# Softmax normalisation on VectorE, stored weight parts, and another order of products in a paired feed-forward layer

## The chip, the cores and the metric

The kernel runs on one core of one Trainium2 chip, in one launch. The metric is the device time of a whole execution in microseconds (us); the median of three runs is shown. All data is fp32. Matrix products run in the TensorE type `fp32r`, and to keep the precision each factor is split into a high part (the value rounded to `fp32r`) and a low part (the rest), so that one product of two factors is three matmuls: high by high, high by low, low by high.

## What is computed

Causal attention over 4 batches, 12 heads, 448 positions and 64 values a head, then a layer norm and a feed-forward layer with a residual:

```python
scores = scale * np.matmul(q, k.transpose(0, 1, 3, 2))
scores = np.where(mask, -1000000000.0, scores)        # mask: above the diagonal
attn = np.exp(scores - np.max(scores, axis=-1, keepdims=True))
attn = attn / (np.sum(attn, axis=-1, keepdims=True) + 1e-09)
x = heads_joined(np.matmul(attn, v))                  # (4, 448, 768)
xn = (x - mu) / np.sqrt(var + 1e-06) * g_ln
out = x + np.maximum(xn @ w_ch1, 0.0) @ w_ch2         # 768 -> 3072 -> 768
```

## The kernel before

All engines run in the order in which the code is written (`manual_schedule`); each engine works its own queue strictly in that order, and waits where an operand is not ready. Time is divided by hand into *slots*: slot s emits 18 feed-forward matmuls (half of a block of the generator `ffn`, one yield), preceded and followed by whatever the tables `pre`, `post` and `ahead` hold for that slot.

**Weights.** The weights arrive as 64-bit floats and are cut into units of 128x768; there are 48 units a batch (`ns`), used one a slot. For batch 0 a unit is loaded raw (`load_raw`), converted in two steps (`convert1` on ScalarE, `convert2` on VectorE, line 129), and kept in device memory as fp32 (`keep`). For batch 1 (slots 48 to 95) `load_full` reads it back. For either, `split1` (ScalarE, line 141) makes the high part `wh` and `split2` (VectorE, line 145) the low part `wl`, two slots and one slot ahead of the use. Each has four buffers.

**Attention.** Batch 0 runs ahead of the slots. Batches 1, 2 and 3 are laid under the slots of batches 0 and 1 by `STARTS`: a pair of heads p begins at its slot t0 and runs scores (TensorE), running maximum and mask (VectorE, line 277), `exps` (ScalarE), `norm`, transposes, and the product with v. `norm` forms 1/sum on VectorE (lines 302 and 303) and multiplies four triangular pieces of 112 rows by 112, 224, 448 and 336 with it (line 307), on GpSimd. Line 238 subtracts the high part of k on GpSimd.

**The pair.** Batches 2 and 3 go through the feed-forward layer together, with seven products for the eight of a 2x2 block product (the Winograd form of Strassen's scheme): the weights give the left factors A11, A12, A22 and the sums S1 to S4, the two batches give the right factors B11, B21, B22 and the differences T1 to T4. `LEFT` and `RIGHT` name which belong to products 1 to 7.

- `inputs(c)` makes the right factors of one of three chunks from the normalised inputs of both batches (`xg`): eight operations for `xg`, four subtractions t1 to t4, and for each of seven factors the high part on ScalarE and the low part on GpSimd or VectorE (`parts`, lines 534 and 535). It is called in slots 87, 90 and 93 (`PAIR` is 86).
- After slot 95 `run` goes over 30 blocks in six groups: two blocks of layer 1 (63 matmuls each, nine a product), then three of layer 2 (42 each, six a product). Product 4 of a layer-2 block is put behind the first product of the next block.
- `load` and `combine` bring a block's weights from device memory and form S1 to S4 on GpSimd (line 627), 15 and 11 products ahead. `weight` splits each of the seven left factors six products ahead (`AHEAD`), high part on ScalarE and low part on VectorE.
- A product accumulates in one of three PSUM banks of its block, A, X or Y. `after1` and `after2` do what follows: partial results are copied to SBUF (p1, p5, u2), added into banks, and in layer 1 turned by ReLU into the right factors of layer 2 (`hid`, high and low); in layer 2 they are added to the residual `xT`.

## Time and profile before

| | us |
|---|---|
| runs | 984.96, 985.91, 987.09; median 985.91 |
| profiled execution | 984.65 |
| its span, first to last instruction | 982.9 |
| busy in the span: TensorE | 887.1 |
| VectorE | 715.0 |
| ScalarE | 531.8 |
| GpSimd | 400.0 |
| mean granted TensorE clock | 0.975 |

An engine's busy time is the union of its instructions' spans. Matmuls overlap: one is shown with 0.37 us, while the next starts 0.20 us after it. So the pace is read from starts, and a wait from the idle time ahead of an instruction and what ended it. Busy shares are averages over stages with different limits, so the span is cut into stages.

### The profile page before, as it was taken

What the parts mean: (1) busy time and instruction counts of PE and PEld (TensorE: products, weight loads), DVE (VectorE), ACT (ScalarE), POOL (GpSimd) and SP (SyncE); (2) the same over time, 40 slices, a digit from 0 to 9 for tenths busy, and PEclk for the clock granted to TensorE, in tenths of its full rate; (3) what the DMA queues carried; (4) which work ended last, traced back from release to release, by engine and by line L of the source; (5) the groups of instructions that cost most, each with busy time, mean ns of one, the idle gap of its engine ahead of it and who ended that gap; (6) DMA issues with size and microseconds to landing.
All of it is one profiled execution on the core that took longest, in us unless ns stands there. A gap on an engine that the chain in (4) does not pass through costs nothing.

```text
span 982.9 us, 13419 instructions
## 1 busy us (share of the span) xinstructions
PE 887.1 (90%) x4662; PEld 757.8 (77%) x4662; DVE 715.0 (73%) x1341; ACT 531.8 (54%) x1176; POOL 400.0 (41%) x447
## 2 busy tenths in 40 slices
...
GB/s 249 320 47 141 170 260 283 287 291 290 245 252 148 194 186 112 112 112 111 123 127 33 85 81 11 52 54 54 42 66 43 54 54 38 70 43 55 54 44 112
DMA packets 35251, 125.51 MB, mean 128 GB/s; under 512 B 4080, under 2 KB 8688, under 8 KB 35184
## 3 DMA queue, kind: packets, MB, share of 16 engines
...
## 4 chain that ended last, share of the span: by engine, by line
PE 52%; DVE 26%; ACT 13%; issue 5%; DMA 3%; SPq 1%; POOL 0%; ACTq 0%; DVEq 0%; POOLq 0%
PE po L493 13%; PE ph L474 13%; DVE wp L535 6%; PE bX L667 6%; PE bY L667 4%; PE bA L667 4%; PE px L342 4%; DVE w L129 3%; PE sc L269 3%; PE pt L323 3%; DVE xT L734 2%; ACT wp L534 2%; DVE t L682 2%; DVE wl L145 2%; ACT P L291 1%
## 5 line engine op out<-in xcount | busy, mean ns | idle before, releaser
L307 POOL TENSOR_SCALAR P<-P,r 112x112 f32<-112x112 f32 (+3 forms) x176 | 110.3, 645 | 275.6 <-DVE r L303 259.4
L493 PE MATMUL po<-hh,wl 128*128 128x448 f32 x288 | 109.0, 379 | 29.7 <-DVE wl L145 29.7
L535 DVE TENSOR_TENSOR wp<-s,wp 128x256 fp32r<-128x256 f32 (+1 forms) x120 | 95.7, 799 | 34.4 <-ACT wp L534 32.2
L291 ACT ACTIVATE P<-P,nm 112x448 f32<-112x448 f32 (+3 forms) x176 | 91.8, 526 | 48.4 <-DVE nm L277 48.2
L493 PE MATMUL po<-hh,wh 128*128 128x448 f32 x288 | 109.5, 380 | 0.0
L493 PE MATMUL po<-hl,wh 128*128 128x448 f32 x288 | 108.1, 375 | 0.0
L474 PE MATMUL ph<-xh,wh 128*128 128x448 f32 x288 | 107.8, 374 | 0.0
L474 PE MATMUL ph<-xh,wl 128*128 128x448 f32 x288 | 106.0, 368 | 1.4 <-DVE wl L145 1.4
L474 PE MATMUL ph<-xl,wh 128*128 128x448 f32 x288 | 105.8, 367 | 0.8 <-POOL xl L409 0.8
L535 DVE TENSOR_TENSOR wp<-u,wp 128x256 fp32r<-128x256 f32 (+1 forms) x90 | 71.6, 796 | 35.5 <-ACT wp L534 35.5
L277 DVE CUSTOM_DVE_ANT_0 P<-sc,mask 112x448 f32<-112x448 f32 (+3 forms) x176 | 70.5, 443 | 30.3 <-PE sc L269 18.3
L493 PEld LDWEIGHTS po<-hh,wl 128*128 128x128 f32 x288 | 56.2, 195 | 36.8 <-DVE wl L145 31.9
L480 DVE SCALAR_TENSOR_TENSOR hl<-ph,hh 128x448 fp32r<-128x448 f32 x48 | 29.8, 622 | 69.7 <-ACT hh L479 69.7
L627 POOL TENSOR_TENSOR s<-u 128x256 f32<-128x256 f32 (+1 forms) x60 | 58.4, 973 | 53.1 <-DVE wp L535 25.3
L129 DVE SCALAR_TENSOR_TENSOR w<-w,bits 128x768 uint32<-128x768 uint32 x48 | 73.7, 1536 | 3.7 <-ACT bits L122 3.5
L667 PE MATMUL bY<-h,wp 128*128 128x448 f32 x216 | 54.3, 381 | 21.0 <-ACT fx L742 15.3
L667 PEld LDWEIGHTS bY<-h,wp 128*128 128x128 f32 x216 | 40.0, 189 | 29.6 <-ACT fx L742 17.6
L145 DVE TENSOR_TENSOR wl<-full,wh 128x768 fp32r<-128x768 f32 x48 | 61.2, 1279 | 1.6 <-ACT wh L141 1.6
L667 PE MATMUL bX<-h,wp 128*128 128x448 f32 x216 | 55.7, 381 | 6.8 <-DVE xT L734 6.8
L323 PE MATMUL pt<-ident,P 112*112 112x112 f32 x440 | 54.8, 261 | 7.1 <-DVE stat L358 3.9
L493 PEld LDWEIGHTS po<-hh,wh 128*128 128x128 f32 x288 | 56.3, 195 | 5.1
L323 PEld LDWEIGHTS pt<-ident,P 112*112 112x112 f32 x440 | 46.3, 133 | 17.3 <-ACT PT L326 3.6
...
## 6 DMA issues: line engine op xcount, KB each, us to landing
...
scratch<-w SPq DMA_DIRECT2D x48, 384.0 KB, 5.1
...
```

The costliest lines, as they stand in the source:

```text
L129: nc.vector.scalar_tensor_tensor(out=w, in0=w, scalar=3, in1=bits.pop(s), op0=ALU.logical_shift_left, op1=ALU.bitwise_or,)
L145: nc.vector.tensor_tensor(out=wl[s], in0=w32[s], in1=wh[s].bitcast(F32), op=ALU.subtract)
L277: nc.vector.tensor_tensor_reduce(out=self.t["P", p, h][:, OFF[i]:OFF[i + 1]], in0=pt[:, o:o + n], in1=mask[:, S - n:], op0=ALU.add, op1=AL ...
L291: nc.scalar.activation(out=pp, in_=pp, func=ACTF.Exp, scale=-1.0, bias=nm[:, x:x + 1], accum_out=self.t["sm", p, h][:, i:i + 1],)
L307: eng.tensor_scalar(out=pp, in0=pp, scalar1=r[:, i:i + 1], scalar2=1.0, op0=ALU.mult, op1=ALU.mult,)
L323: nc.tensor.transpose(pt[:, o:o + C], pp[:, a:a + C], ident[:C, :C])
L342: nc.tensor.matmul(px[D * h:D * h + D, C * j:], lhsT=vt[:, h, j, :], rhs=self.t.pop(("PT", p, h, j)), start=(j == 0), stop=(j == NC - 1),)
L474: nc.tensor.matmul(pm[y], lhsT=w[:, c * P:c * P + P], rhs=z[:, c, :], start=(c == 0 and i == 0), stop=(c == KC - 1 and i == 2),)
L493: nc.tensor.matmul(pm, lhsT=w[:, o:o + P], rhs=z[:, x, :], start=(x == 0 and i == 0), stop=(x == HF - 1 and i == 2),)
L535: eng.tensor_tensor(out=lo, in0=src, in1=hi.bitcast(F32), op=ALU.subtract)
L627: nc.gpsimd.tensor_tensor(out=v[out], in0=x, in1=y, op=op)
L667: nc.tensor.matmul(pm, lhsT=w, rhs=z, start=(new and c == 0 and i == 0), stop=(c == nk - 1 and i == 2), skip_group_check=True,)
```

## The change

Four things change.

1. `norm` multiplies on VectorE for batches 1 to 3 instead of GpSimd, and the attention of batches 2 and 3, with the pair's start, is two slots earlier.
2. Each rounded unit of slots 36 to 83 is also stored as its two parts (`keep_parts`, two DMAs). Units 84 to 95 are read back as parts (`load_parts`) instead of being read and split. In the pair the left factors A11, A12 and A22 are read as parts (`weight_parts`, one DMA) and only S1 to S4 are split.
3. The pair's inputs come in twelve portions, one in each of slots 84 to 95, instead of three lumps; B11 and B21 use the buffers of `xh` and `xl`.
4. In the pair product 1 accumulates in bank X with 6, 7 and 4; layer 1 keeps its differences in the banks A, Y and a fourth, Z, instead of SBUF; parts of the work behind products 3 and 4 are put off by one or two products (`then`); layer 2 adds each bank's running value into `xT` on VectorE, without copies. The products stand in another order.

The diff, cut (of functions that were rewritten mostly the new lines are shown; the old ones stand above):

```diff
-STARTS[2] = [32 + 4 * p for p in range(6)]
-STARTS[3] = [56 + 4 * p for p in range(6)]
+STARTS[2] = [30 + 4 * p for p in range(6)]
+STARTS[3] = [54 + 4 * p for p in range(6)]
-PAIR = 86
-LEFT = {1: "A11", 2: "A12", 3: "S4", 4: "A22", 5: "S1", 6: "S2", 7: "S3"}
+PAIR = 84
+KEEP0 = 36
+LEFT = {1: (0, 0), 2: (0, 1), 3: "S4", 4: (1, 1), 5: "S1", 6: "S2", 7: "S3"}
-ORDER1, ORDER2 = [1, 6, 5, 2, 7, 3, 4], [1, 5, 6, 3, 2, 7, 4]
+ORDER1, ORDER2 = [1, 2, 6, 5, 7, 3, 4], [1, 5, 6, 3, 7, 2, 4]
...
+    def load_parts(s):
+        for part, w, tag in ((0, wh, "wh"), (1, wl, "wl")):
+            t = sb.tile([P, UH], F32, tag=tag, name=tag, bufs=4)
+            nc.sync.dma_start(out=t, in_=kept[s % ns][:, part, :])
+            w[s] = t.bitcast(F32R)
+    def keep_parts(s):
+        for part, w in ((0, wh), (1, wl)):
+            nc.sync.dma_start(out=kept[s % ns][:, part, :], in_=w[s].bitcast(F32))
...
 
         put(ns, (open_late, None))
         for s in range(2 * ns):
+            if s >= ns + KEEP0:
+                put(s - 3, (load_parts, s))
+                continue
             t = (-EARLY + GAP * s, *ELAG) if s < early else (s - 4, 1, 2, 3)
             put(t[0] + t[3], (split2, s))
+            if s >= KEEP0:
+                put(s, (keep_parts, s))
...
-        rank = [open_late, split2, convert2, convert1, keep, load_raw, load_full, split1]
+        rank = [open_late, split2, convert2, convert1, keep, load_raw, load_full, keep_parts, load_parts, split1]
...
         def parts(self):
-            self.xh = xp.tile([P, KC, S], F32R, tag="xh", name="xh", bufs=1)
-            self.xl = xp.tile([P, KC, S], F32R, tag="xl", name="xl", bufs=1)
+            self.xh = sb.tile([P, KC, S], F32R, tag="xh", name="xh", bufs=1)
+            self.xl = sb.tile([P, KC, S], F32R, tag="xl", name="xl", bufs=1)
...
-            eng = nc.vector if self.b == 0 and p >= NDVE else nc.gpsimd
+            eng = nc.vector if self.b or p >= NDVE else nc.gpsimd
...
+            self.at[0].parts()
             self.xo = {
                 (op, part): self.xp.tile([P, KB, S], F32R, tag=f"x{op}{part}", name=f"x{op}{part}")
-                for op in RIGHT.values() for part in "hl"
+                for op in RIGHT.values() for part in "hl" if op not in ("B11", "B21")
             }
+            for k, op in enumerate(("B11", "B21")):
+                for part, t in (("h", self.at[0].xh), ("l", self.at[0].xl)):
+                    self.xo[op, part] = t[:, k * KB:(k + 1) * KB, :]
+            self.f = {}
...
+        def xg(self, c, k, j):
...
+            nc.vector.tensor_tensor(out=t, in0=a.xT[cc], in1=a.t["mb"], op=ALU.subtract)
+            nc.vector.scalar_tensor_tensor(
+                out=t, in0=t, scalar=g_sb[:, cc:cc + 1], in1=a.t["rb"], op0=ALU.mult, op1=ALU.mult,
+            )
...
+        def xsub(self, c, name, x, y):
+            self.f[c, name] = t = self.tmp(name)
+            nc.vector.tensor_tensor(out=t, in0=self.f[(c, *x)], in1=self.f[(c, *y)], op=ALU.subtract)
+        def xparts(self, c, op, x, eng):
+            self.parts(self.f[(c, *x)], self.xo[op, "h"][:, c, :], self.xo[op, "l"][:, c, :], eng)
+
         def inputs(self, c):
...
+            G, V = nc.gpsimd, nc.vector
+            return [
+                [(self.xg, c, 0, 0), (self.xparts, c, "B11", (0, 0), G), (self.xg, c, 0, 1)],
+                [(self.xg, c, 1, 1), (self.xsub, c, "t1", (0, 1), (0, 0)), (self.xsub, c, "t2", (1, 1), ("t1",)),
+                 (self.xparts, c, "T2", ("t2",), G)],
+                [(self.xg, c, 1, 0), (self.xparts, c, "B21", (1, 0), G), (self.xparts, c, "T1", ("t1",), V)],
+                [(self.xsub, c, "t3", (0, 1), (1, 1)), (self.xparts, c, "T3", ("t3",), G),
+                 (self.xsub, c, "t4", (1, 0), ("t2",)), (self.xparts, c, "B22", (1, 1), G),
+                 (self.xparts, c, "T4", ("t4",), V)],
+            ]
...
-            for n in range(len(self.items)):
-                self.todo.setdefault(n - AHEAD, []).append((self.weight, n))
-            self.u, self.s, self.w, self.bank, self.hid = {}, {}, {}, {}, {}
+            for n, (b, k) in enumerate(self.items):
+                if isinstance(LEFT[k], tuple):
+                    self.todo.setdefault(n - AHEAD, []).append((self.weight_parts, n))
+                else:
+                    self.todo.setdefault(n - AHEAD, []).append((self.weight, n))
...
+        def weight_parts(self, n):
+            b, k = self.items[n]
+            w, (i, kk) = self.width(b), LEFT[k]
+            s, o = self.unit(b, i)
+            o += kk * w
+            s, o = s + o // UH, o % UH
+            t = sb.tile([P, 2, w], F32, tag=("wh", "wl")[n % 2], name="wk", bufs=4)
+            nc.sync.dma_start(out=t, in_=kept[s][:, :, o:o + w])
+            self.w[b, k] = t.bitcast(F32R)
...
         def weight(self, n):
+            w, src = self.width(b), self.u[b][LEFT[k]]
+            self.w[b, k] = t = sb.tile([P, 2, w], F32R, tag=("wh", "wl")[n % 2], name="wp", bufs=4)
+            nc.scalar.activation(out=t[:, 0, :], in_=src, func=ACTF.Copy)
+            nc.vector.tensor_tensor(
+                out=t[:, 1, :], in0=src, in1=t[:, 0, :].bitcast(F32), op=ALU.subtract
+            )
...
-            name = {1: "A", 2: "A", 6: "X", 7: "X", 4: "X", 5: "Y", 3: "Y"}[k]
+            name = {1: "X", 2: "A", 6: "X", 7: "X", 4: "X", 5: "Y", 3: "Y"}[k]
-            (self.after1 if blk[0] == 1 else self.after2)(b, blk, k)
...
+            def rest(op, src, eng=V):
+                minus(lo(op), src, hi(op).bitcast(F32), eng)
+
+            def then(lag, f, *args):
+                self.later.setdefault(self.n + lag, []).append((f, args))
...
             if k == 1:
-                nc.scalar.copy(out=self.p1, in_=bank["A"])
+                self.p1 = self.tmp("p1")
+                copy(self.p1, X)
             elif k == 6:
-                V.tensor_tensor(out=bank["X"], in0=bank["X"], in1=self.p1, op=ALU.add)
                 self.u2 = self.tmp("u2")
-                nc.scalar.copy(out=self.u2, in_=bank["X"])
+                copy(self.u2, X)
+            elif k == 2:
+                plus(A, A, self.p1)
+                self.b11 = self.tmp("b11")
+                copy(hi("B11"), A, ACTF.Relu)
+                copy(self.b11, A, ACTF.Relu)
+                rest("B11", self.b11, G)
             elif k == 5:
-                nc.scalar.copy(out=self.p5, in_=bank["Y"])
-                V.tensor_tensor(out=bank["Y"], in0=bank["Y"], in1=self.u2, op=ALU.add)
...
+                self.p5 = self.tmp("p5")
+                copy(self.p5, Y)
+                plus(Y, Y, self.u2)
             elif k == 7:
+                Z = self.psum(b, "Z")
+                plus(Z, X, self.p5)
                 self.b22 = self.tmp("b22")
...
+                copy(hi("B22"), Z, ACTF.Relu)
+                copy(self.b22, Z, ACTF.Relu)
+                rest("B22", self.b22, G)
             elif k == 3:
...
+                relu_minus(A, Y, self.b11)
+                minus(Z, self.b22, A)
+                copy(hi("T1"), A)
+                copy(hi("T2"), Z)
+                relu_minus(Y, Y, self.b22)
+                rest("T1", A)
+                rest("T2", Z)
+                then(1, copy, hi("T3"), Y)
+                then(2, rest, "T3", Y)
             elif k == 4:
...
+                b21 = self.tmp("b21")
+                copy(b21, X, ACTF.Relu)
+                copy(hi("B21"), X, ACTF.Relu)
+                rest("B21", b21, G)
+                then(1, minus, Z, b21, Z)
+                then(1, copy, hi("T4"), Z)
+                then(2, rest, "T4", Z)
...
-            def add(i, j, src, eng):
...
+            def add(i, j, src):
                 m = 2 * blk[2] + i
                 t = self.at[j].xT[m]
-                eng.tensor_tensor(out=t, in0=t, in1=src, op=ALU.add)
+                nc.vector.tensor_tensor(out=t, in0=t, in1=src, op=ALU.add)
...
-            if k == 1:
-                nc.scalar.copy(out=self.p1, in_=bank["A"])
-            elif k == 5:
-                nc.scalar.copy(out=self.p5, in_=bank["Y"])
-            elif k == 6:
-                V.tensor_tensor(out=bank["X"], in0=bank["X"], in1=self.p1, op=ALU.add)
-                add(0, 1, bank["X"], V)
-                add(1, 1, self.p5, G)
-            elif k == 3:
-                add(0, 1, bank["Y"], V)
-            elif k == 2:
-                add(0, 0, bank["A"], V)
-            elif k == 7:
-                add(1, 1, bank["X"], V)
-            elif k == 4:
-                add(1, 0, bank["X"], V)
+            add(*{
+                1: (0, 0, X), 5: (1, 1, Y), 6: (0, 1, X), 3: (0, 1, Y), 7: (1, 1, X), 2: (0, 0, A), 4: (1, 0, X),
+            }[k])
 
...
             for n, (b, k) in enumerate(self.items):
                 self.product(b, k)
                 self.before(n)
+                self.n = n
+                (self.after1 if self.blocks[b][0] == 1 else self.after2)(b, self.blocks[b], k)
+                for f, args in self.later.pop(n, []):
+                    f(*args)
...
-                elif (s - PAIR) % 3 == 1 and (s - PAIR) // 3 < KB:
-                    pair.inputs((s - PAIR) // 3)
+                    steps = [x for c in range(KB) for x in pair.inputs(c)]
+                for f, *args in steps.pop(0) if steps else []:
+                    f(*args)
```

VectorE's queue where the pair's inputs begin to be made, before: the end of the first lump (`t`: t1 to t4; `xT2l`, `xT4l`: low parts), then the low parts of three feed-forward units.

```order
L544 SCALAR_TENSOR_TENSOR xg<-xg,g_sb,rb 128x448
L543 TENSOR_TENSOR xg<-xT,mb 128x448
L544 SCALAR_TENSOR_TENSOR xg<-xg,g_sb,rb 128x448
L554 TENSOR_TENSOR t_5793<-xg 128x448
L554 TENSOR_TENSOR t_5795<-xg 128x448
L554 TENSOR_TENSOR t_5805<-xg,t_5793 128x448
L554 TENSOR_TENSOR t_5807<-xg,t_5805 128x448
L535 TENSOR_TENSOR xT2l<-t_5805,xT2h 128x448
L535 TENSOR_TENSOR xT4l<-t_5807,xT4h 128x448
L145 TENSOR_TENSOR wl<-full,wh 128x768 x2
L497 TENSOR_TENSOR xT<-po,xT 128x448
L145 TENSOR_TENSOR wl<-full,wh 128x768
```

The same queue after, from the second portion on (`L513` is the feed-forward's addition, `L561` and `L562` make `xg`, `L568` the differences, `L556` low parts):

```order
L513 TENSOR_TENSOR xT<-po,xT 128x448
L561 TENSOR_TENSOR xg<-xT,mb 128x448
L562 SCALAR_TENSOR_TENSOR xg<-xg,g_sb,rb 128x448
L568 TENSOR_TENSOR t_5877<-xg 128x448
L568 TENSOR_TENSOR t_5879<-xg,t_5877 128x448
L561 TENSOR_TENSOR xg<-xT,mb 128x448
L562 SCALAR_TENSOR_TENSOR xg<-xg,g_sb,rb 128x448
L556 TENSOR_TENSOR xT1l<-t_5877,xT1h 128x448
L513 TENSOR_TENSOR xT<-po,xT 128x448
L568 TENSOR_TENSOR t_5937<-xg 128x448
L568 TENSOR_TENSOR t_5941<-xg,t_5879 128x448
L556 TENSOR_TENSOR xT4l<-t_5941,xT4h 128x448
```

The input operations now stand in short pieces between the feed-forward's additions, and no low parts of units stand behind them.

VectorE's queue where the second layer-1 block of a group ends and layer 2 begins, before (`wp`: low part of a left factor; `t<-bX,t` and `h<-bX,h`: T4 and B21 behind product 4; `bX<-bX,fx`, `xT`: layer 2):

```order
L535 TENSOR_TENSOR wp<-u_6613,wp 128x256
L682 SCALAR_TENSOR_TENSOR t_6863<-bX,t_6836 128x448
L682 SCALAR_TENSOR_TENSOR h_6111<-bX,h_6111 128x448
L535 TENSOR_TENSOR wp<-s,wp 128x256
L535 TENSOR_TENSOR wp<-u_6719,wp 128x256
L535 TENSOR_TENSOR wp<-u_6613,wp 128x256
L744 TENSOR_TENSOR bX<-bX,fx 128x448
L734 TENSOR_TENSOR xT<-xT,bX 128x448
L535 TENSOR_TENSOR wp<-s,wp 128x256
L734 TENSOR_TENSOR xT<-xT,bY 128x448
L535 TENSOR_TENSOR wp<-s,wp 128x256
L734 TENSOR_TENSOR xT<-xT,bA 128x448
```

The same place after (`L709`, `L714`: T1, T2, T3 behind product 3 and their low parts `h` and `hx`; `bZ`: T4; `L779`: additions into `xT`):

```order
L709 SCALAR_TENSOR_TENSOR bA<-bY,b_6388 128x448
L714 TENSOR_TENSOR bZ<-b_6442,bA 128x448
L709 SCALAR_TENSOR_TENSOR bY<-bY,b_6442 128x448
L714 TENSOR_TENSOR h_6235<-bA,h_6235 128x448
L714 TENSOR_TENSOR hx<-bZ,hx 128x448
L779 TENSOR_TENSOR xT<-xT,bX 128x448
L714 TENSOR_TENSOR hx<-bY,hx 128x448
L714 TENSOR_TENSOR bZ<-b_6479,bZ 128x448
L779 TENSOR_TENSOR xT<-xT,bY 128x448
L714 TENSOR_TENSOR h_6235<-bZ,h_6235 128x448
L660 TENSOR_TENSOR wp<-s,wp 128x256
L779 TENSOR_TENSOR xT<-xT,bX 128x448
```

The additions of layer 2 now begin between the low parts of T2, T3 and T4, and low parts of left factors are fewer.

ScalarE's queue from product 3 of the first layer-1 block to the first copy of the second block (`fx<-bA` of line 687, the copy p1), before:

```order
L534 ACTIVATE wp<-u_7534 128x384
L534 ACTIVATE h_6110<-t_7713 128x448
L534 ACTIVATE h_6110<-t_7714 128x448
L534 ACTIVATE h_6111<-t_7715 128x448
L534 ACTIVATE wp<-s 128x384
L719 ACTIVATE h_6110<-bX 128x448
L534 ACTIVATE h_6110<-t_7741 128x448
L534 ACTIVATE wp<-s 128x384
L687 COPY fx<-bA 128x448
```

The same place after (`p_7342<-bX` is the copy p1, `h_6234<-bZ` behind it the high part of T4):

```order
L706 ACTIVATE h_6234<-bA 128x448
L706 ACTIVATE h_6234<-bZ 128x448
L659 ACTIVATE wp<-s 128x384
L706 ACTIVATE b_7325<-bX 128x448
L706 ACTIVATE h_6234<-bX 128x448
L706 ACTIVATE h_6235<-bY 128x448
L706 ACTIVATE p_7342<-bX 128x448
L706 ACTIVATE h_6234<-bZ 128x448
```

The copy p1 moved ahead of the high part of T4, and one high part of a left factor is between instead of three.

## Rows read from the trace of the kernel before

**Rows 1.** By stage: us, busy of PE, PEld, DVE, ACT, POOL, PEclk, DMA share, GB/s
```profile
60.00:543.00 483.00, 465.89 (x2672) 400.46 (x2673) 340.90 (x708) 301.67 (x629) 148.71 (x179) 1.00 0.49 178
543.00:613.00 70.00, 43.49 (x197) 38.99 (x196) 47.57 (x57) 17.67 (x33) 31.83 (x24) 0.80 0.15 53
613.00:979.40 366.40, 327.89 (x1513) 286.44 (x1511) 285.12 (x435) 166.54 (x384) 183.51 (x177) 0.98 0.17 55
```

**Rows 2.** Timeline, TensorE in the pair (start, us, engine, line, op): pace
```profile
737.65 0.36 PE L667 MATMUL bX<-xT2h,wp 128*128 128x448 f32 x1
...
739.49 0.36 PE L667 MATMUL bY<-xT1h,wp 128*128 128x448 f32 x1
```

**Rows 3.** Timeline, TensorE between 546 and 613 us
```profile
546.60 0.45 PE L493 MATMUL po<-hh,wh 128*128 128x448 f32 x1
...
610.20 0.57 PE L493 MATMUL po<-hh,wh 128*128 128x448 f32 x1
...
610.57 0.57 PE L493 MATMUL po<-hl,wh 128*128 128x448 f32 x1
...
612.95 0.36 PE L667 MATMUL bA<-xB11h,wp 128*128 128x448 f32 x1
```

**Rows 4.** Waits of TensorE, 543 to 613 us: total, times, longest
```profile
PE po L493 <- DVE wl L145: 26.5, 3, 10.4
```

**Rows 5.** Waits of TensorE, 613 to 983 us
```profile
PE bY L667 <- ACT fx L742: 15.3, 6, 2.6
PE bA L667 <- ACT fx L687: 8.7, 6, 1.6
PE bX L667 <- DVE xT L734: 6.8, 13, 1.2
PE bY L667 <- DVE h L535: 5.7, 6, 1.0
```

**Rows 6.** Timeline, VectorE in the first input lump
```profile
560.68 1.55 DVE L535 TENSOR_TENSOR xT4l<-t,xT4h 128x448 fp32r<-128x448 f32 x1
```

**Rows 7.** Groups of the pair: busy us, mean ns of one, idle before
```profile
L535 DVE TENSOR_TENSOR wp<-u,wp 128x256 fp32r<-128x256 f32 (+1 forms) x90 | 71.6, 796 | 35.5 <-ACT wp L534 35.5
...
L734 DVE TENSOR_TENSOR xT<-xT,bA 128x448 f32<-128x448 f32 x18 | 11.0, 608 | 0.1
...
L682 DVE SCALAR_TENSOR_TENSOR t<-bY,b 128x448 f32<-128x448 f32 x24 | 14.7, 611 | 0.0
...
L535 DVE TENSOR_TENSOR h<-t,h 128x448 fp32r<-128x448 f32 x18 | 10.5, 610 | 0.0
...
L693 ACT COPY fx<-bY 128x448 f32<-128x448 f32 x12 | 6.4, 531 | 1.6 <-PE bY L667 1.6
```

**Rows 8.** DMA issues from 255 to 340 us: KB each, median us to landing
```profile
scratch<-w SPq DMA_DIRECT2D x11, 384.0 KB, 4.5
```

**Rows 9.** Timeline, VectorE at the border into layer 2
```profile
701.56 1.26 DVE L535 TENSOR_TENSOR wp<-s,wp 128x256 fp32r<-128x256 f32 x1 [1.69 <-ACT wp L534]
...
704.77 0.61 DVE L535 TENSOR_TENSOR h<-t,h 128x448 fp32r<-128x448 f32 x1
...
705.30 0.61 DVE L535 TENSOR_TENSOR hx<-t,hx 128x448 fp32r<-128x448 f32 x1
```

**Rows 10.** VectorE groups by shape, and by line (ns min/median/max), up to 545 us
```profile
L129 DVE SCALAR_TENSOR_TENSOR w<-w,bits 128x768 uint32<-128x768 uint32 x44 | 69.7, 1584 | 2.5 <-ACT bits L122 2.2
...
L129 DVE SCALAR_TENSOR_TENSOR w<-w,bits x48: 927/952/4694, 16.2 to 319.6; 128x768 uint32<-128x768 uint32 x48
...
L228 DVE CAST kh<-qkraw 128x896 fp32r<-128x896 f32 x17 | 10.3, 609 | 0.0
...
L302 DVE TENSOR_SCALAR r<-sm x48: 156/162/336, 12.2 to 511.0; 112x4 f32<-112x4 f32 x48
...
L277 DVE CUSTOM_DVE_ANT_0 P<-sc,mask 112x448 f32<-112x448 f32 x36 | 22.2, 618 | 6.8 <-PE sc L269 6.8
```

**Rows 11.** Waits of TensorE, 60 to 543 us
```profile
PE po L493 <- DVE wl L145: 3.1, 3, 1.7
```

145 lines of the change are left out of this document (48 added, 97 removed).

## Prediction

> **What bounds the kernel now.** I read three views in this order: the table by stage, the waits of TensorE in each stage, then the rows around the longest waits. The table [rows 1] cuts the span at 543 us (the pair's input work begins) and 613 us (the pair's first product). From 60 to 543 us TensorE is busy 465.9 of 483 us: that stage is bound by TensorE's own work. From 543 to 613 us it is busy 43.5 of 70, while VectorE is busy 47.6: TensorE waits for VectorE there. From 613 to 979.4 us it is busy 327.9 of 366.4, and VectorE 285.1.
>
> How much can be won is read from the pace. Nine matmuls of one product take 739.49 - 737.65 = 1.84 us [rows 2], 0.2044 each. *Transition:* after the row at 546.60 us nine slots of 18 feed-forward matmuls follow until 612.95 us [rows 3]; at that pace they need 162 x 0.2044 = 33.1 us and take 66.4, so 33 us are lost. [...] *Pair:* 1512 matmuls at 0.2044 need 309.1 us; from 612.95 us to the last one, 0.37 us before the stage's end at 979.4, it takes 366.1, so 57 us are lost. The waits name 36.5 of them [rows 5]: for a ScalarE copy of a partial product (15.3 and 8.7), for a VectorE addition in place (6.8), for a hidden low part (5.7). The rest is restart steps and the lower clock behind the longest of them (granted 0.98 over the stage).
>
> **The change, part by part.**
>
> *1. The pair's inputs.* Before, the inputs of two 128-row chunks came as one lump of 14 VectorE operations, in slots 87, 90 and 93, ahead of the `wl` of the next feed-forward units (first order rows). The subtractions and low parts in it take 1.55 us [rows 6] where the same shape takes 0.610 alone [rows 7]: GpSimd works on its own low parts at that moment. Now the same operations stand in twelve portions, one a slot, and no `wl` is behind them: units 84 to 95 come as stored parts by DMA, so 12 ScalarE and 12 VectorE operations go. A slot lasts 18 x 0.2044 = 3.7 us. Per four slots VectorE has four pairs of about 1.25 us (two starts 0.6 apart), four subtractions and two low parts of 0.61 to 1.55, two additions of 0.62: 9.9 to 15.5 us for 14.7. It fits in the middle, and it may run late without harm, since nothing that TensorE wants before 613 us is in this queue now except two additions behind three PSUM buffers. What comes late next is the first product that needs the last portion's T3 or B22, four products (7 us) into the pair; their chain (addition, subtraction, ScalarE copy, GpSimd low part: 0.62 + 0.61 + 0.58 + 1.4 = 3.2 us) is covered. I take -32 of the 33 lost; bounds -33 and -22 (one wait of 10 us kept).
>
> *2. The 90 products on stored parts.* For A11, A12 and A22 the high part (ScalarE) and the low part (VectorE, 90 x 0.796 = 71.6 us [rows 7]) are replaced by one DMA each, six products ahead (7.4 us and more). Landing of the nearest transfer, 384 KB to the store, is 4.5 us [rows 8]; the queues move 55 GB/s in this stage [rows 1], and the loads add 28 MB in some 318 us, 89 GB/s. Hidden, by 3 us; without that cover each would cost its lateness.
>
> *3. Products 1, 6, 7 and 4 accumulate in one bank, and layer 2 adds each partial bank into `xT` on VectorE.* Gone are layer 2's copies p1 and p5 (36 on ScalarE), 18 additions `bX<-bX,fx`, 18 additions on GpSimd. VectorE does 126 additions instead of 91: +35 x 0.608 [rows 7] = +21 us; layer 1 has 11 operations a block instead of 10: +7 us; the 18 additions -11; with -72 from step 2 VectorE is busy about 285 - 55 = 230 of some 318 us. It is no bound on average, as before; what counts is who waits for which operation. A layer-2 product of six matmuls lasts 1.23 us. Its bank is written again two products later; the result is there 0.37 - 0.20 us after the last start, the addition takes 0.61, so TensorE could go on 0.9 us into the product between: no wait in the steady part. In layer 1 the worst chain is product 5, copy p5 (0.53 [rows 7]), addition of u2 (0.61), then product 3 with nine matmuls of product 7 between: 0.17 + 0.53 + 0.61 and three gaps of 0.06, 1.5 of 1.84 us. The copy p5 of layer 2 (15.3) no longer exists. The copy p1 that product 2 waited for (8.7) stood behind T4's ScalarE copy, which waits for VectorE; now it stands ahead of it (third order rows), but only one product lies between it and product 6, which needs it.
>
> *4. The border into layer 2.* Here a wait comes in. Layer 1's last products leave, in VectorE's order (second order rows), the five operations behind product 3 and then, mixed, two additions and three operations for T3 and T4. Set 0 at the start of product 3 of the second block: its result is there at 2.0 us, or VectorE is free at 2.7 to 3.4 us, because the low part of S3 (0.43 alone, 1.2 to 1.4 beside GpSimd) stands ahead and itself waits for two ScalarE copies. The five go on at a step of 0.53 to 0.60 [rows 9]: T1's low part is ready at 5.2 to 5.8, wanted at 5.8; the addition of product 1's bank is done at 6.3 to 7.0, wanted at 6.2; that of product 5 at 8.0 to 8.7, wanted at 7.4 plus the first delay. So 0.5 to 1.2 us, and about 0.4 at the next addition, are lost in each of six groups: 5 to 10 us, I take 8. On the border from the first to the second layer-1 block the same queue delays ScalarE: copies of T1 and T2, a weight's high part, B21 twice, T3, then p1, seven of 0.42 to 0.58 from 3.4 to 4.0 on, so p1 is there at 6.7 to 7.9 and wanted at 7.4: 0 to 0.5 a group, 2 us in all. Pair: 309.1 + 10 = 319 us, -47; bounds -54 (3 left) and -28 (half of the 57 left).
>
> [...] VectorE operations of 128x448 take 0.610 us on SBUF alone (`h<-t,h`), 0.611 from PSUM and SBUF (`t<-bY,b`) and 0.608 (`xT<-xT,bA`) [rows 7]. So I charge nothing for temporaries in PSUM. [...]
>
> *5. Normalising on VectorE (batches 1 to 3), attention two slots earlier.* 144 multiplications go from GpSimd to VectorE. The trace has none on VectorE: at least 0.162 (four elements, line 302), at most 0.618 (line 277, 448 elements). Nearest is line 228, one SBUF input, 896 elements in 0.609 (median 0.611) [rows 10]; on the line through it and 0.162 the widths 112 to 448 give 0.22, 0.27, 0.33, 0.39, so 1.2 us a head and 43 us in all (23 to 64 by the bounds). Against it: line 129 takes 0.952 in the median, 1.584 in the mean and 4.694 at most [rows 10], the long ones while GpSimd runs four such multiplications and the subtraction of line 238. 44 x 0.63 = 28 us of VectorE go with them at most. VectorE: 341 + 43 - 28 = 356 of 483 us, not a bound. TensorE's waits for `wl` in line 493 are 3.1 us here [rows 11]; I take -4 for these and lesser ones, bounds -10 and +10 (the other side is step 6). Two slots earlier changes nothing on a saturated TensorE.
>
> *6. Stores of the parts.* 48 units, two DMAs of 384 KB each, 38 MB in the last 60% of this stage: some 130 GB/s on the 178 there [rows 1]. They hold the four buffers of `wh` and `wl` until they land. Unit s+4 is written on ScalarE two slots after the store's issue (about 11 us, a slot with attention being some 5.5), against 4.5 us landing. Cost 0, by that cover; within the +10.
>
> **Sum.** Profiled execution 984.65 us (span 982.9 and 1.75 around it): -4 - 32 - 47 = 901.7. The median of the runs, 985.91, lies 1.3 above the profiled one: **903 us**. All bounds good: 888; all bad: 946.
>
> **Rivals.**
> (a) *VectorE's queue at the borders stays the bound.* For: it is busy four fifths of the pair, and low parts double beside GpSimd. Against: 72 us less of these, and the waits of [rows 5] are for copies that go. Half the 57 us stay: 18 us more than my sum, 921.
> (b) *No wait at the borders* (low parts at 0.43): 10 us less, and the attention's gain whole, 6 more: 887.
> (c) *Slower: stores hold ScalarE.* If a part lands later than the 11 us plus two slots of lead, the high part of unit s+4 is late, ScalarE's queue behind it (hidden layers, exponentials) stands still and TensorE waits in each of 48 units. It decides from about 20 us of landing, four times the 4.5; it loses all of the gain at 83 / 48 = 1.7 us a unit, and at 2 us gives 903 + 96 = 999. For: loads, old stores and new ones meet while batch 0 is still being converted. Against: the mean rate.
> [...]
>
> **Chances.** My forecast (893 to 913) 0.60, (b) 0.11, (a) 0.13, (d) 0.07, two of these together (931 to 980) 0.04, (c) 0.05. The range, 888 to 931, leaves out the last two and little of (b). A measurement here can tell about 0.2% from no change. Faster 0.94, same 0.01, slower 0.05.
>
> **What would show it.** Step 1: no wait for `wl` over 3 us after 530 us, and granted clock 1.0 there. Steps 2 and 3: the pair takes 310 to 328 us from first product to last; no TensorE wait for a layer-2 copy. Step 4: the waits left stand at products 6, 3 and 7 of the first layer-2 block of a group, for `xT` additions. Step 5: line 129's longest near 2 to 3 us, multiplications near 0.3 us. Step 6: ScalarE shows no wait for a store. I am wrong if TensorE waits for a stored part's DMA, or if the stage before 543 us is longer by over 10 us.

## The result, and the profile after

The changed kernel takes **920.89 us** (median of four runs, 918.47 to 922.83) against 985.43 of the kernel before beside it: ratio 0.9345, 95% interval 0.9316 to 0.9374. The forecast was 903 with 888 to 931: sign and range are right, the point is 18 us too low. The profiled execution took 918.47 us (span 916.6), so 66.2 us are gained where the sum had 83.

The windows of the changed kernel that answer to [rows 1] (columns as there; the cuts are now the pair's input work at 543 us and the pair's first product at 586):

```profile
60.00:543.00 483.00, 460.04 (x2660) 397.33 (x2659) 354.17 (x847) 297.20 (x624) 69.13 (x36) 0.99 0.71 255
543.00:586.00 43.00, 43.00 (x219) 39.25 (x219) 29.99 (x45) 10.57 (x20) 21.70 (x18) 1.00 0.66 227
586.00:913.10 327.10, 316.85 (x1513) 281.00 (x1511) 224.97 (x382) 123.69 (x277) 150.22 (x154) 1.00 0.47 146
```

The transition is now full: TensorE is busy 43.00 of 43.00 us. The pair is 39 us shorter and runs at a granted clock of 1.00. The first stage is the surprise: TensorE is busy 460.04 us where it was busy 465.89 in the same 483. To split the 66 us I use the timeline of TensorE: the first matmul of feed-forward slot 84 (all attention lies before it, but for four short statistics in the kernel before), the first and the last matmul of the pair. In the changed kernel the first two are

```profile
537.75 0.45 PE L509 MATMUL po<-hh,wh 128*128 128x448 f32 x1
...
585.97 0.37 PE L695 MATMUL bX<-xh,wk 128*128 128x448 f32 x1
```

and the last matmul starts at 912.62 us. In the kernel before they are at 531.59, 612.95 and 979.01.

| stretch | before | after | difference | forecast |
|---|---|---|---|---|
| start to slot 84 | 531.6 | 537.8 | +6.2 | -4 |
| slot 84 to the pair's first product | 81.4 | 48.2 | -33.2 | -32 |
| first to last matmul of the pair | 366.1 | 326.7 | -39.4 | -47 |

So the miss stands in two places: 10 us in the attention, where even the sign is wrong, and 8 in the pair. The waits of TensorE (total, times, longest) show where. The first line below reads: TensorE (PE) at line 339, for its tile `pt`, waited 5.5 us in three pieces, 2.4 the longest, for VectorE's `stat` of line 374 (DVE is VectorE, ACT ScalarE, POOL GpSimd, SPq SyncE's queue, PEclk the granted clock). From 200 to 345 us in the changed kernel, the longest four:

```profile
PE pt L339 <- DVE stat L374: 5.5, 3, 2.4
PE pln L371 <- ACT PT L342: 4.1, 2, 3.7
PE pt L339 <- ACT PT L342: 3.6, 3, 2.6
PE pln L371 <- ACT xT L362: 1.1, 1, 1.1
```

All waits there are 16.1 us against 8.7 before. Only 0.2 us of them are for `wl` (compare [rows 11]); 13.9 are for the PSUM banks `pt` that transposes (`pt`) and statistics (`pln`) share. And in the pair, from 582 us on (to compare with [rows 5]):

```profile
PE bX L695 <- ACT p L706: 5.7, 7, 2.9
PE bX L695 <- DVE xT L779: 2.3, 6, 0.4
PE bY L695 <- DVE xT L779: 1.5, 6, 0.3
```

The layer-2 copies of [rows 5] are gone. By steps between matmuls (what each is longer than 0.207 us) the pair loses 18.1 us instead of 56.9: 7.6 at product 6 of layer 1 (3.1 in the first block of a group, 4.5 in the second) and 10.5 at products 5, 6, 3 and 7 of the first layer-2 block; the 14 steady layer-2 products of a group lose nothing.

### The profile page after: what moved, and what is told of

Same layout as the page of the kernel before. It is cut to its first block, busy times and chain, and to the rows that moved or that the text cites. A ratio compares the mean times of both kernels' runs of the same rounds, so it can differ in the third digit from the quotient of the medians.

```text
span 916.6 us, 13600 instructions
## 1 busy us (share of the span) xinstructions
PE 869.5 (95%) x4662; PEld 749.8 (82%) x4662; DVE 649.8 (71%) x1412; ACT 476.7 (52%) x1050; POOL 275.7 (30%) x274
## 4 chain that ended last, share of the span: by engine, by line
PE 63%; ACT 14%; DVE 14%; DMA 4%; issue 4%; SPq 1%; POOL 0%; ACTq 0%; DVEq 0%
PE ph L490 15%; PE bX L695 14%; PE po L509 13%; PE bY L695 6%; PE px L358 4%; PE bA L695 3%; PE sc L285 3%; PE pt L339 3%; ACT P L307 2%; DVE wp L660 2%; ACT h L706 2%; DMA scratch<-w 2%; DVE w L136 1%; ACT w L125 1%; ACT b L706 1%
## 5 line engine op out<-in xcount | busy, mean ns | idle before, releaser
L254 POOL TENSOR_TENSOR kl<-qkraw,kh 128x896 fp32r<-128x896 f32 x18 | 49.3, 2740 | 294.6 <-DVE kh L244 224.6
L509 PE MATMUL po<-hh,wh 128*128 128x448 f32 x288 | 106.9, 371 | 0.0
L509 PE MATMUL po<-hh,wl 128*128 128x448 f32 x288 | 105.8, 367 | 0.2 <-DVE wl L156 0.2
L660 DVE TENSOR_TENSOR wp<-s,wp 128x256 fp32r<-128x256 f32 (+1 forms) x120 | 76.8, 645 | 33.8 <-ACT wp L659 32.2
L659 ACT ACTIVATE wp<-s 128x256 fp32r<-128x256 f32 (+1 forms) x120 | 53.7, 459 | 86.4 <-PE bY L695 41.9
L714 POOL TENSOR_TENSOR h<-b,h 128x448 fp32r<-128x448 f32 x36 | 41.3, 1148 | 126.8 <-ACT b L706 82.2
L779 DVE TENSOR_TENSOR xT<-xT,bX 128x448 f32<-128x448 f32 x72 | 44.6, 619 | 34.5 <-PE bX L695 33.9
L490 PEld LDWEIGHTS ph<-xl,wh 128*128 128x128 f32 x288 | 54.7, 190 | 5.6 <-POOL xl L425 1.3
L490 PEld LDWEIGHTS ph<-xh,wh 128*128 128x128 f32 x288 | 54.7, 190 | 4.9
L490 PEld LDWEIGHTS ph<-xh,wl 128*128 128x128 f32 x288 | 54.5, 189 | 4.6 <-DVE wl L156 0.3
```

The source lines that it names most:

```text
L254: nc.gpsimd.tensor_tensor(out=kl, in0=rk, in1=kh.bitcast(F32), op=ALU.subtract)
L490: nc.tensor.matmul(pm[y], lhsT=w[:, c * P:c * P + P], rhs=z[:, c, :], start=(c == 0 and i == 0), stop=(c == KC - 1 and i == 2),)
L509: nc.tensor.matmul(pm, lhsT=w[:, o:o + P], rhs=z[:, x, :], start=(x == 0 and i == 0), stop=(x == HF - 1 and i == 2),)
L659: nc.scalar.activation(out=t[:, 0, :], in_=src, func=ACTF.Copy)
L660: nc.vector.tensor_tensor(out=t[:, 1, :], in0=src, in1=t[:, 0, :].bitcast(F32), op=ALU.subtract)
L714: eng.tensor_tensor(out=dst, in0=src, in1=y, op=ALU.subtract)
```

## Experiments

Each kernel is the changed one with one edit. The last three columns are, from its trace, the time of slot 84's first matmul, from there to the pair, and the pair. The code up to slot 84 is alike in runs 5 to 11; their slot 84 lies at 537.1 to 539.3 us, in run 5's trace at 542.8, so a single trace carries an error of up to 2 us there, and once 5 (run 5's trace is its slowest execution, 927.2 us).

| run | edit | median us | ratio to before (95%) | slot 84 | to pair | pair |
|---|---|---|---|---|---|---|
| - | the change | 920.9 | 0.9345 (0.9316-0.9374) | 537.8 | 48.2 | 326.7 |
| 1 | attention at the old slots | 913.4 | 0.9262 (0.9242-0.9281) | 525.8 | 49.3 | 332.1 |
| 2 | normalising on GpSimd | 923.7 | 0.9371 (0.9350-0.9392) | 543.4 | 48.2 | 327.1 |
| 3 | no stores of parts | 919.3 | 0.9333 (0.9305-0.9361) | 538.2 | 48.2 | 326.9 |
| 4 | only batch 2's first pairs at the old slots | 926.1 | 0.9384 (0.9357-0.9411) | 543.9 | 48.2 | 327.8 |
| 5 | inputs in three lumps | 922.0 | 0.9360 (0.9324-0.9396) | 542.8 | 48.3 | 330.4 |
| 6 | slots 84 to 95 split as before | 930.0 | 0.9418 (0.9395-0.9442) | 539.3 | 56.4 | 328.9 |
| 7 | pair's weights all split | 967.2 | 0.9812 (0.9793-0.9831) | 537.1 | 48.2 | 375.6 |
| 8 | products 1, 2, 5, 6 | 926.4 | 0.9391 (0.9368-0.9414) | 538.5 | 48.3 | 334.8 |
| 9 | weights seven ahead | 927.7 | 0.9414 (0.9392-0.9436) | 537.8 | 48.2 | 334.8 |
| 10 | the same, B21's copies later | 921.6 | 0.9353 (0.9330-0.9375) | 537.1 | 48.2 | 330.7 |
| 11 | weights behind the banks' operations | 924.8 | 0.9377 (0.9363-0.9391) | 538.2 | 48.2 | 332.1 |
| 12 | old slots, inputs in 8 slots | **911.2** | 0.9238 (0.9225-0.9251) | 527.7 | 52.3 | 325.2 |

### Where the attention lost 10 us: runs 1 to 4

**Run 1.** Attention of batches 2 and 3 at the old slots; the twelve portions then have ten slots.

```diff
-STARTS[2] = [30 + 4 * p for p in range(6)]
-STARTS[3] = [54 + 4 * p for p in range(6)]
-PAIR = 84
+STARTS[2] = [32 + 4 * p for p in range(6)]
+STARTS[3] = [56 + 4 * p for p in range(6)]
+PAIR = 86
...
-                for f, *args in steps.pop(0) if steps else []:
+                for f, *args in steps.pop(0) + (steps.pop(0) if s in (89, 93) else []) if steps else []:
```

> The changed kernel with one part undone: the attention of batches 2 and 3 starts at slots 32 and 56 again and the pair's input work at slot 86, so that its 12 portions fill 10 slots (two portions each in slots 89 and 93). Normalising stays on VectorE, the stores stay. The changed kernel took 920.9 us; between slots 28 and 84 TensorE waited 19.4 us there against 8.8 in the kernel before. Theory A (the two slots make batch 2's first pairs meet the end of batch 1 and the weight conversion): the waits fall to about 9 us and the time to about 911, and the first 28 slots keep their gain of 6 us. Theory B (the multiplications on VectorE make it late, wherever the pairs stand) and theory C (the stores): the waits stay near 19 us, the time within 917 to 924.

Measured 913.4 us, slot 84 at 525.8 instead of 537.8, TensorE's idle time between slots 28 and 84 down from 19.5 to 9.8 us (9.6 before the change): theory A. With the old slots the stage is 5.8 us shorter than before the change, near the -4 that I had forecast. That the time is 913 and not 911 comes from the pair's start (see run 12).

The place is slots 30 to 36. The window of the changed kernel from its slot 30 to its slot 36:

```profile
226.10:270.20 44.10, 35.56 (x195) 30.93 (x194) 33.26 (x73) 28.92 (x57) 5.94 (x2) 0.92 0.65 226
```

The same slots in run 1:

```profile
227.20:256.90 29.70, 29.41 (x172) 25.93 (x170) 23.90 (x52) 23.94 (x46) 2.95 (x1) 1.00 0.83 286
```

And in the kernel before:

```profile
230.80:260.70 29.90, 29.61 (x172) 25.94 (x169) 22.48 (x46) 24.07 (x46) 7.06 (x9) 1.00 0.81 285
```

Six slots take 44.1 us instead of 29.7. Some 23 more matmuls are done in them, but TensorE idles 8.5 us instead of 0.3, and the granted clock falls to 0.92. VectorE is busy 33.26 of 44.1, so it is not full. The timelines of the changed kernel in slots 30 and 31 show what happens instead. VectorE:

```profile
227.34 2.78 DVE L136 SCALAR_TENSOR_TENSOR w<-w,bits 128x768 uint32<-128x768 uint32 x1
...
232.18 1.19 DVE L323 TENSOR_SCALAR P<-P,r 112x112 f32<-112x112 f32 x4
233.28 0.95 DVE L136 SCALAR_TENSOR_TENSOR w<-w,bits 128x768 uint32<-128x768 uint32 x1
...
235.03 0.61 DVE L293 CUSTOM_DVE_ANT_0 P<-sc,mask 112x448 f32<-112x448 f32 x1
```

ScalarE:

```profile
235.68 0.67 ACT L307 ACTIVATE P<-P,nm 112x448 f32<-112x448 f32 x1 [3.05 <-DVE nm L293]
...
237.27 0.89 ACT L125 ACTIVATE w<-raw 128x768 f32<-128x768 f32 x1
238.07 0.86 ACT L129 ACTIVATE bits<-raw 128x768 uint32<-128x768 uint32 x1
238.84 0.82 ACT L152 ACTIVATE wh<-w 128x768 fp32r<-128x768 f32 x1
239.57 0.52 ACT L495 ACTIVATE hh<-ph 128x448 fp32r<-128x448 f32 x1
239.99 0.94 ACT L342 COPY PT<-pt 112x448 f32<-112x448 f32 x2
```

TensorE:

```profile
231.23 0.45 PE L285 MATMUL sc<-kh,qs 128*112 128x448 f32 x1
...
235.89 0.93 PE L339 MATMUL pt<-ident,P 112*112 112x112 f32 x8
240.56 0.68 PE L371 MATMUL pln<-ident,xT 128*112 128x128 f32 x2 [3.75 <-ACT PT L342]
```

Batch 2's first scores are started at 231.23 us. Their reduction stands in VectorE's queue behind four multiplications and a conversion, which an earlier conversion of 2.78 us had already put off, and begins at 235.03. The exponentials stand at the head of ScalarE's queue and hold it for 3.05 us. Behind them come the conversion of a weight unit and a hidden layer, and only then the copies of batch 1's last transposes, at 239.99. TensorE, which wants that bank for batch 1's statistics, waits 3.75 us. In run 1 the first scores come two slots later. The same copies run at once, ahead of the exponentials (ScalarE, run 1):

```profile
235.85 0.96 ACT L342 COPY PT<-pt 112x448 f32<-112x448 f32 x2
236.69 0.93 ACT L125 ACTIVATE w<-raw 128x768 f32<-128x768 f32 x1
...
242.38 0.67 ACT L307 ACTIVATE P<-P,nm 112x448 f32<-112x448 f32 x1 [0.44 <-DVE nm L293]
```

So a new pair's scores, the old batch's last transposes and statistics, and the weight conversion met in the same slots, through three queues that each work in order. This chain explains the 3.75 us; most of the other idle time in these slots, two waits of 2.4 and 1.7 us in slots 34 and 35, is for the statistics on VectorE (`stat`), and what held those is not followed here.

**Run 2.** Normalising back on GpSimd.

```diff
-            eng = nc.vector if self.b or p >= NDVE else nc.gpsimd
+            eng = nc.gpsimd
```

> The changed kernel with the 144 multiplications of batches 1 to 3 back on GpSimd; all else stays. Theory B (VectorE is late because of them): TensorE's waits of 19.4 us between slots 28 and 84 fall to about 9, and the 6 us that slots 0 to 28 gained are lost again: 917 us; if the multiplications did not give the 6 us either, 911. Theory A (the two slots): the waits stay near 19 us, the 6 us are lost: 927 us. Theory C (the stores) expects the same 927.

Measured 923.7 us; the runs of the two kernels don't overlap (923.1 to 925.6 against 918.5 to 922.8), though the intervals do. Slot 28 comes at 221.0 us instead of 214.3, slot 84 at 543.4 instead of 537.8: with 1.3 us taken off for a later start, normalising on VectorE gains 5.4 us up to slot 28 and 4.3 up to slot 84 (with a trace's error of about 2; the medians differ by 2.8). TensorE's waits for `wl` from 60 to 540 us are 3.6 us here, 4.5 before the change and 0.2 with it. The idle time between slots 28 and 84 stays at 17.1 us. Theory B is out as the main cause; of the 19.5 us it may carry 2 or 3.

**Run 3.** No stores; the loads read the unrounded weights.

```diff
-            if s >= KEEP0:
-                put(s, (keep_parts, s))
...
-            nc.sync.dma_start(out=t, in_=kept[s % ns][:, part, :])
+            nc.sync.dma_start(out=t, in_=scratch[s % ns // 2][:, part * UH:(part + 1) * UH])
...
-            nc.sync.dma_start(out=t, in_=kept[s][:, :, o:o + w])
+            nc.sync.dma_start(
+                out=t, in_=scratch[s // 2].rearrange("p (i c) -> p i c", i=2)[:, :, o:o + w]
+            )
```

> The changed kernel without its 96 stores of rounded parts; the loads of parts read the same number of bytes from the unrounded weights instead, so the weights of slots 84 to 95 and of the pair's products 1, 2 and 4 are not the right ones, and the time is that of the kernel without the stores. Theory C (the stores take DMA time that the weight loads and the buffers of the parts need): the 11 us of extra waits between slots 28 and 84 go, 910 us. Theories A and B: the stores lie hidden, 919 to 922 us, the waits at 222 to 269 us, which stand before the first store, unchanged at 10 us.

Measured 919.3, an interval that overlaps the changed kernel's almost whole; slot 84 at 538.2, the wait of 3.8 us in slot 31 unchanged. Theory C is out: the 38 MB lie hidden.

**Run 4.** Only batch 2's first five pairs at the old slots, its sixth squeezed in.

```diff
-STARTS[2] = [30 + 4 * p for p in range(6)]
+STARTS[2] = [32, 36, 40, 44, 48, 51]
```

> The changed kernel with batch 2's pairs at slots 32, 36, 40, 44, 48 and 51 instead of 30, 34, ... 50; batch 3 stays at 54, the pair's inputs at slot 84. So only the first five pairs stand where they stood before the change, and the last one is squeezed in. If the 12 us that the stage lost come from batch 2's first pairs meeting the end of batch 1 in slots 28 to 36 (the run with both batches two slots later reached slot 84 at 525.8 us instead of 537.8), they come back without the 5 us that that run lost at the pair's start: slot 84 at 526 to 528 us, 909 to 911 us in all. Rival: the whole attention, with the weight conversion up to slot 44, is too dense for ScalarE's and VectorE's queues, and the wait is only put off to the squeezed pair: slot 84 at 533 or later, 916 and up.

Measured 926.1: the rival. Slot 48 comes at 329.2 us, 14.8 ahead of the changed kernel, and slot 60 at 418.6, 5.5 behind it. Windows from slot 49 on, over 364 matmuls; run 4:

```profile
334.50:413.00 78.50, 66.34 (x364) 56.30 (x362) 50.69 (x133) 35.98 (x89) 7.16 (x3) 0.91 0.60 217
```

Run 1:

```profile
335.90:397.00 61.10, 60.52 (x364) 52.41 (x363) 46.42 (x122) 34.68 (x84) 8.13 (x3) 1.00 0.78 284
```

The conversion is over there, VectorE is busy two thirds of the time and ScalarE under half; still TensorE waits 11.4 us for `PT` copies in the attention of this run, up to 5.4 us at a time. So the conversion is not needed for such waits; pairs that stand closer are enough. From batch 1's last pair to batch 2's first, while the weights are converted, the kernel before has six slots and loses 0.3 us of TensorE in slots 30 to 36; the changed kernel has four and loses 8.5. From batch 2 to batch 3, after the conversion, four slots go with at most 1.3 us at a time, and the three of run 4 do not. That does not make the distance alone the rule: inside batch 2 the pairs of run 1 stand four slots apart while the conversion still runs, and TensorE's longest wait there is 1.9 us. What the end of a batch adds to it (its last transposes and its statistics) was not varied by itself.

### What removed the 33 us of the transition: runs 5 and 6

**Run 5.**

```diff
-                for f, *args in steps.pop(0) if steps else []:
+                for f, *args in sum([steps.pop(0) for _ in range(4)], []) if s % 4 == 1 and steps else []:
```

> The changed kernel with the pair's inputs in three lumps of four portions (slots 85, 89 and 93) instead of twelve portions, one a slot; the weights of slots 84 to 95 still come as stored parts. Theory H (the 33 us of the transition went because no low part of a feed-forward unit stands behind the inputs any more): TensorE waits nowhere between 545 us and the pair, and only the last lump may make the pair's first products late: 921 to 925 us. Theory I (the portions did it): a lump of some 12 us of VectorE stops TensorE in two or three places by 8 us or more: 937 and up.

**Run 6.**

```diff
-            if s >= ns + KEEP0:
-                put(s - 3, (load_parts, s))
-                continue
...
-            if s >= KEEP0:
+            if KEEP0 <= s < KEEP0 + ns:
                 put(s, (keep_parts, s))
```

> The changed kernel with the weights of slots 84 to 95 loaded and split as before (12 high parts on ScalarE, 12 low parts on VectorE); the inputs stay in twelve portions, the stores stay. Theory H (the stored parts did it, a low part behind the inputs is late): waits for a low part of 8 us or more between 545 and 586 us, 929 and up. Theory I (the portions did it: a low part stands behind one portion only): less than 3 us of waits, 920 to 924.

Lumps with stored parts: 922.0 us, 48.3 from slot 84 to the pair, the same as with portions; the last lump costs 3.6 us at the first block's product 7. Portions without stored parts: 930.0 us, 56.4, with low parts late again (waits of TensorE in run 6, 543 to 600 us):

```profile
PE po L506 <- DVE wl L156: 5.1, 4, 2.0
```

So the stored parts without the portions give all of the 33 us, the portions without the stored parts 25 of them (81.4 - 56.4). Run 5 is theory H. In run 6 the time is H's, but the waits are 5.1 us where H asked for 8 and I for less than 3; the other 3 us of the 8.2 that this stretch is longer are in no wait, by estimate in slower steps: the granted clock was 0.987 over this execution, 0.994 over the changed kernel's. So H names what finished the job, not the only thing that could do most of it, and with stored parts the portions add nothing that these runs can tell. Both runs keep the input work two slots earlier; run 1, with stored parts and the old start, needs 49.3 us, so the earlier start is worth about 1. The wider spacing of the lumps (four slots instead of three) was not tested by itself.

### What the pair's 39 us rest on: runs 7 to 11

**Run 7.**

```diff
-                if isinstance(LEFT[k], tuple):
+                if False:
                     self.todo.setdefault(n - AHEAD, []).append((self.weight_parts, n))
...
-            self.u[b] = v
+            self.u[b] = {**u, **v}
```

> The changed kernel with products 1, 2 and 4 of the pair taking their weights as before: 90 more high parts on ScalarE and low parts on VectorE, no loads of stored parts there (the stores stay). Theory F (the pair's 39 us come from the order of the products and from the copies that are gone, the stored parts only lie beside it): the pair takes up to 5 us more than 326.7, 921 to 926 us. Theory G (they come from VectorE's 72 us less): VectorE has some 300 of 327 us again, the operations at the borders stand behind low parts, and the pair takes 15 us more or over: 936 and up.

Measured 967.2 us: theory G, and by far more than it asked. The pair takes 375.6 us, 9.5 more than before the change. Its window:

```profile
585.00:961.00 376.00, 336.39 (x1515) 295.70 (x1513) 281.12 (x471) 159.40 (x369) 155.66 (x155) 0.94 0.16 54
```

TensorE's waits in it:

```profile
PE bX L695 <- DVE xT L779: 14.0, 7, 2.3
PE bX L695 <- ACT p L706: 11.1, 7, 5.9
PE bY L695 <- DVE xT L779: 7.3, 6, 1.5
PE bX L695 <- ACT u L706: 6.6, 6, 1.1
```

VectorE is busy 281 of 376 us, as little full as before the change, and TensorE waits at the borders all the same. 56 us of VectorE work and 36 us of high parts on ScalarE cost 49 us of time: the waits, and the granted clock of 0.94, which by estimate is worth up to 0.06 x 376 = 23 us. Without the stored parts the new order and banks are a loss in the pair. Two things stay open: which of the two engines' work costs more (21.3 us of these waits are for VectorE, 17.7 for ScalarE's copies), and what the stored parts would give with the old order and banks, which was not run.

**Run 8.**

```diff
-ORDER1, ORDER2 = [1, 2, 6, 5, 7, 3, 4], [1, 5, 6, 3, 7, 2, 4]
+ORDER1, ORDER2 = [1, 2, 5, 6, 7, 3, 4], [1, 5, 6, 3, 7, 2, 4]
...
                 copy(self.u2, X)
+                plus(Y, Y, self.u2)
...
                 copy(self.p5, Y)
-                plus(Y, Y, self.u2)
```

> The changed kernel with layer 1's products in the order 1, 2, 5, 6, 7, 3, 4 instead of 1, 2, 6, 5, 7, 3, 4, and the addition of u2 moved behind product 6. Now two products instead of one lie between product 1 and product 6, which needs the copy p1 out of its bank. If the 7.6 us that TensorE loses at product 6 of layer 1 (3.1 in the first block of a group, 4.5 in the second) are only the lateness of that copy, they go: 913 us. Rival: ScalarE's and VectorE's queues at the border are late as a whole, and the wait turns up at product 3 (which needs the addition of u2) or in layer 2's first block: 918 to 921 us.

Measured 926.4, slower by 5.5: neither theory. The wait for p1 falls from 5.7 to 1.1 us, and 9.2 us in twelve waits for the copy `u` come: product 7 now follows product 6 in the same bank and needs it copied out. I had looked at the one copy and not at the next one of that bank.

**Runs 9 and 10.**

```diff
-NTMP, AHEAD = 6, 6
+NTMP, AHEAD = 6, 7
```

> The changed kernel with the pair's weights made (or loaded) seven products ahead instead of six. At the border into layer 2 this takes the split of S3, whose low part took VectorE 1.10 us beside GpSimd and held product 3's five operations (they began at 722.80 us, 1.27 after the product's result), out of product 3's place; at the border between the two layer-1 blocks it puts S4's split there instead. Theory D (that low part sets the 10.5 us that TensorE waits in the first layer-2 block of the six groups): about 6 us go there, product 6 of layer 1 keeps its 7.6: 914 to 916 us. Theory E (the seven operations themselves are too many for the time): less than 2 us go, 919 to 921.

```diff
-                copy(b21, X, ACTF.Relu)
-                copy(hi("B21"), X, ACTF.Relu)
-                rest("B21", b21, G)
-                then(1, minus, Z, b21, Z)
-                then(1, copy, hi("T4"), Z)
-                then(2, rest, "T4", Z)
+                then(1, copy, b21, X, ACTF.Relu)
+                then(1, copy, hi("B21"), X, ACTF.Relu)
+                then(1, rest, "B21", b21, G)
+                then(2, minus, Z, b21, Z)
+                then(2, copy, hi("T4"), Z)
+                then(3, rest, "T4", Z)
```

> The edit of the run before, and ScalarE's two copies of product 4's bank (for B21) behind the copy p1 of the next product instead of ahead of it, with T4's operations one product later. If p1 is late only because seven copies stand in ScalarE's queue (the last one before it ended at 713.41 us, 1.7 after product 1's result), the 4.5 us at product 6 of the second layer-1 block fall below 1 as well; the 3.1 us of the first block, 3.03 of which fall on the very first one, stay: 910 to 912 us. Rival: the queue's head waits for VectorE (2.44 us at the border), and what is moved back is missed at T4 in layer 2: no less than the run before.

**Run 11.**

```diff
                 self.product(b, k)
-                self.before(n)
                 self.n = n
...
                 for f, args in self.later.pop(n, []):
                     f(*args)
+                self.before(n)
```

> The changed kernel with the split (or load) of the weights six products ahead put behind the operations on a product's bank instead of ahead of them. At both borders the low part that takes 1.10 to 1.20 us beside GpSimd then stands behind product 3's five operations, which begin 1.2 us earlier, and every addition of layer 2 stands ahead of a low part. Nothing leaves VectorE. Theory D' (the order in the queue sets the waits): the second block's product 6 loses less than 1 us instead of 4.5 in the six groups, the first layer-2 block 6 instead of 10.5: 912 to 914 us. Theory E (the work between product 3 and layer 2's fourth product is too much for VectorE, 8.16 of 8.6 us busy): what is won at one product is lost at the next, as in the two runs with another distance: 919 to 923 us.

Measured 927.7, 921.6 and 924.8 us: none is faster than the change. What VectorE does at the border of the changed kernel, third group (product 3's result is there at 721.5 us):

```profile
721.77 1.10 DVE L660 TENSOR_TENSOR wp<-s,wp 128x256 fp32r<-128x256 f32 x1 [1.42 <-ACT wp L659]
722.80 0.62 DVE L709 SCALAR_TENSOR_TENSOR bA<-bY,b 128x448 f32<-128x448 f32 x1
...
725.76 0.61 DVE L779 TENSOR_TENSOR xT<-xT,bX 128x448 f32<-128x448 f32 x1
...
727.50 0.61 DVE L779 TENSOR_TENSOR xT<-xT,bY 128x448 f32<-128x448 f32 x1
```

From 722.5 to 731.1 us it is busy 8.16 of 8.60. With the weights seven ahead the low part of 1.10 us is gone from there, and the five operations begin right after the product's result; but another weight's split now stands ahead of product 5's addition and itself waits for ScalarE (run 9, same border):

```profile
730.22 0.62 DVE L779 TENSOR_TENSOR xT<-xT,bX 128x448 f32<-128x448 f32 x1
...
732.94 0.47 DVE L660 TENSOR_TENSOR wp<-s,wp 128x256 fp32r<-128x256 f32 x1 [0.91 <-ACT wp L659]
733.33 0.61 DVE L779 TENSOR_TENSOR xT<-xT,bY 128x448 f32<-128x448 f32 x1
```

The loss at products 5 and 6 of the first layer-2 block goes from 5.3 us to 0, that at product 3 from 3.1 to 9.9. Most of run 9's time is lost elsewhere: layer 1 loses 14.3 us instead of 7.6, 6.3 of them at product 6 of the first block and 4.2 at product 7 of the second. In run 10 the second block's product 6 loses nothing any more (4.5 before), and product 7 loses 5.1 and layer 2's product 7 7.6 instead of 2.1. In run 11 product 6 loses 6.7 in the second layer-1 block and 5.9 in the layer-2 one, where it lost 4.5 and 3.9. None of the three times lies in a range that was expected; run 9 and run 11 are slower than theory E had it, and run 10, which takes 6 us off run 9, is no faster than the change. In kind it is theory E: of the orders tried here none helps, what is won at one product is lost at another. That VectorE is too full for any order is argued from the 8.16 of 8.60 us, not shown.

### A faster version: run 12

The starts of the batches as in run 1, and

```diff
-PAIR = 84
+PAIR = 86
...
-                for f, *args in steps.pop(0) if steps else []:
+                for f, *args in steps.pop(0) + (steps.pop(0) if s % 2 else []) if steps else []:
```

> The attention of batches 2 and 3 and the pair's inputs two slots later, as in the run that undid that part (913.4 us), but the twelve portions stand one and two in turn in slots 86 to 93 instead of 86 to 95. In that run the last portion's operations stood on VectorE behind the addition of the last feed-forward product, its three ScalarE copies ahead of the copy p1, and TensorE lost 7.7 us at product 6 of the first block and 0.7 at the pair's first product. If that is the last portion's lateness alone, these fall to about 1 us, the stage up to slot 84 stays 12 us shorter than in the changed kernel, and the time is 905 to 907 us. Rival: two portions in every other slot hold VectorE so long that additions of the feed-forward products are late and TensorE waits in slots 87 to 94: 912 us and up.

Measured 911.2 us, between the two expectations; it is 9.7 below the changed kernel and the fastest here, though its interval overlaps the end of run 1's. The pair takes 325.2 us instead of 332.1, so the last portion was the cause of run 1's loss there. Not foreseen was the first product, which waits for its stored part. TensorE's waits in run 12 from 560 us on:

```profile
PE bX L695 <- DMA wk<-kept: 3.6, 1, 3.6
```

VectorE and SyncE's queue in run 12, just ahead of that product:

```profile
574.54 0.62 DVE L568 TENSOR_TENSOR t<-xg,t 128x448 f32<-128x448 f32 x1
575.09 0.62 DVE L513 TENSOR_TENSOR xT<-po,xT 128x448 f32<-128x448 f32 x1
...
575.73 0.34 SPq L515 DMA_DIRECT2D out_dram<-xT  x1
576.17 1.21 SPq L652 DMA_DIRECT2D wk<-kept  x2
```

The load (`wk`) stands in SyncE's queue behind the output of the last feed-forward row but one, which waits for that row's addition (line 513); the operations of a double portion stand ahead of the addition on VectorE. The load is issued at 576.17 us, when TensorE has its last feed-forward matmul at 576.05; in run 1 it is issued at 569.66, 5.4 us ahead of the pair. That wait is most of the 5 us by which the run missed its expectation.

## Why the prediction was right, and where not

**Step 1, inputs and stored parts: right** (-33.2 against -32). The 33 us were 26.5 us of waits for `wl` [rows 4] and the slower steps behind them, 0.37 us instead of 0.20, at a granted 0.50 from 602 to 612 us and 0.80 over the stretch [rows 1]. No `wl` wait is left after 530 us, the granted clock is 1.00. One sentence in it fell: late portions do harm. I looked at the products that need T3 and B22; what came late is the copy p1, behind the last portion's three ScalarE copies: 2.9 of the 5.7 us of waits for it are this one wait.

**Step 2, hidden loads: right, and undervalued.** The loads land in 3.8 and 3.2 us (estimate 4.5), no product of the changed kernel waits for one; run 12 shows how thin the cover is. I had VectorE's 72 us in the sum only as a queue that is shorter; run 7 shows that without the stored parts, which also spare ScalarE 36 us, nothing of the pair's gain is left.

**Step 3: right.** No steady wait, no layer-2 copy.

**Step 4, the border: right in place, too small in size.** The first layer-2 block lost 10.5 us where I took 8 (5 to 10), the copy p1 7.6 where I took 2. VectorE's five operations began 1.27 us behind the product's result, within the 0.7 to 1.4 that I had set; but I let the second layer-1 block's product 6 be late by 0 to 0.5, while the whole of ScalarE's queue was late with it: 0.75 a group. The 3.1 us in the first blocks, nearly all of them the late input portion of step 1, I had not counted at all.

On temporaries in PSUM the trace bears out that nothing was charged. `bA<-bY,b`, `bZ<-b,bA` and `h<-bA,h` take 619, 629 and 625 ns in the mean; `t<-xg` of line 568, with SBUF alone, has a median of 620.

**Step 5, normalising on VectorE: right by itself, wrong in its last sentence.** Groups of VectorE in the changed kernel from 60 to 540 us (busy us, mean ns of one, idle before):

```profile
L136 DVE SCALAR_TENSOR_TENSOR w<-w,bits 128x768 uint32<-128x768 uint32 x44 | 48.2, 1095 | 2.5 <-ACT bits L129 2.2
...
L323 DVE TENSOR_SCALAR P<-P,r 112x448 f32<-112x448 f32 x36 | 17.9, 498 | 0.0
...
L323 DVE TENSOR_SCALAR P<-P,r 112x336 f32<-112x336 f32 x36 | 14.0, 389 | 0.0
...
L323 DVE TENSOR_SCALAR P<-P,r 112x224 f32<-112x224 f32 x36 | 11.9, 331 | 0.0
...
L323 DVE TENSOR_SCALAR P<-P,r 112x112 f32<-112x112 f32 x36 | 10.0, 279 | 1.3
```

One of GpSimd, from the page of the changed kernel:

```profile
L254 POOL TENSOR_TENSOR kl<-qkraw,kh 128x896 fp32r<-128x896 f32 x18 | 49.3, 2740 | 294.6 <-DVE kh L244 224.6
```

The multiplications cost 53.8 us (I took 43), some 60 ns more each. The 498 ns of the widest is a mean: its median is 448, and two of the 36 took 1.36 us (see the rivals below). The conversion gives back 21.5 us (69.7 [rows 10] to 48.2; 67.8 in run 2), its longest is 2.78 us instead of 4.69, beside `kl` on GpSimd. VectorE is busy 354 us, forecast 356. The gain is 4.3 us by run 2's trace and 2.8 by its median, forecast 4, and of the waits for `wl` that I had named 0.2 us are left. The step that failed is "Two slots earlier changes nothing on a saturated TensorE": by run 1 it costs 12 us up to slot 84, and 7.5 in the whole time. The stage is saturated only as long as each bank comes free in time: in slots 30 to 36 TensorE idles 8.5 us, in run 1 0.3. The price of that sentence was to be found in the order of the queues in slots 30 to 36, which I did not look at. The +6.2 us of this stage lie inside my bound of +10, but I had set that bound for the stores of step 6: that it held is luck.

**Step 6: right in the cost, wrong in the landing.** The stores land in 8.3 to 8.5 us, not 4.5, so of the 11 us of cover 2.5 are left; ScalarE waits for one once, 0.7 us, and run 3 gains no more than 1.6.

**The rivals.** The time is that of (a), but not its reason alone: VectorE at the borders carries 8 of the 18 us. (b) fell with it. (c) is out by run 3. (d), a VectorE that saturates in the attention, named the right stage and the wrong cause: VectorE is no fuller there than forecast (busy 354 us, forecast 356). No run shows a multiplication and a `kl` subtraction that hold each other: none of the 18 `kl` of the changed kernel lies beside a multiplication. They take 2.74 us in the mean, against 2.11 in run 2, beside other VectorE work (`qs`, the conversion, `wl`); TensorE does not wait for them. Two of the 144 multiplications are long, each begun 0.08 us after a subtraction `xl` on GpSimd. One of them is in this group of four, which lasts 2.10 us instead of the 1.19 above:

```profile
311.22 2.10 DVE L323 TENSOR_SCALAR P<-P,r 112x112 f32<-112x112 f32 x4
...
311.59 1.18 POOL L425 TENSOR_TENSOR xl<-xg,xh 128x448 fp32r<-128x448 f32 x1 [4.17 <-ACT xh L422]
```

Each of the two is 0.91 us longer than the median of its width; no other multiplication is.
